# Twelve matmuls with unused results between the last V tiles of a decode attention kernel

## The chip, the cores and the metric

The kernel runs on one core of a Trainium2 chip (trn2). The metric is the device time of one execution in microseconds (us), given as the median of several. A profile comes from one of these executions. Its span runs from the first to the last instruction and is about 1.8 us shorter than the device time of that execution. In the profile PE is TensorE, PEld its weight loads, DVE VectorE, ACT ScalarE and POOL GpSimd; L192 is line 192 of the kernel. PSUM is the memory in which the kernel keeps the outputs of its matmuls (its pools with `space=bass.MemoryType.PSUM`).

## The reference

Attention for one new token: 32 query heads, 8 key/value heads (four query heads share one), 65536 positions, head size 128, all in bf16.

```python
B, Hq, Hkv, Sq, Sk, D = 1, 32, 8, 1, 65536, 128
k = jnp.repeat(k, rep, axis=1); v = jnp.repeat(v, rep, axis=1)   # rep = 4
scores = jnp.einsum("bhqd,bhkd->bhqk", q, k) * D ** -0.5
p = jax.nn.softmax(scores, axis=-1)
return jnp.einsum("bhqk,bhkd->bhqd", p, v)
```

K and V together are 268 MB, and every byte is used once. Little arithmetic is done per byte.

## The kernel before

The work goes group by group (one group is one K/V head). Each head's K and its V are read in four tiles of 4 MB each, called (g, s) below. So (7,0), (7,1), (7,2) and (7,3) are the last V tiles of the program. Five buffers hold tiles in flight. VectorE transposes K, TensorE forms the scores S, ScalarE takes the exponential, and TensorE multiplies with V. The very last tile is loaded in five pieces, so that little remains to be done once its last bytes land.

```python
iopool = ctx.enter_context(tc.tile_pool(name="iopool", bufs=5))
pss = ctx.enter_context(tc.tile_pool(name="pss", bufs=1, space=bass.MemoryType.PSUM))

CUTS = (T // 2, 3 * T // 4, 7 * T // 8, T - T // 16)      # T = 128 slots
EDGE = CUTS[-1]

def v_step(g, j):
    vt = load(v_view[g, j], "vt")
    # ...
    for c0 in range(0, CW, NQ):
        for u in range(2):
            wide(A[u], E, j, vh[u], u, c0, start=..., stop=...)   # 4 matmuls, 32 in all

def last_step(g, j):
    vt = load(v_view[g, j], "vt", CUTS)
    # ...
    W = pss.tile([P, HI * D], fp32, name="W", tag="S")
    first = halves(vt, 1)[0]
    for c0 in range(0, CW, NQ):                           # first half of the tile: 16 matmuls
        wide(W, E, j, first, 0, c0, start=(c0 == 0), stop=(c0 == CW - NQ))
    Rw = stats.tile([P, D], fp32, name="Rw")
    diagonal([(0, W)], Rw[:, :])                          # VectorE
    nc.vector.tensor_add(out=Rw[:, :], in0=Rw[:, :], in1=R[:, :D])
    # ...
    for t in range(CUTS[0], EDGE):                        # 56 small matmuls into Dp
        slot(t, Dp[s * QP:s * QP + HPG, :], ...)
    nc.vector.tensor_add(out=Ds[:, :], in0=Dp[:, :], in1=Rw[:, :])
    for t in range(EDGE, T):                              # 8 small matmuls into ps_f
        slot(t, ps_f[:, :], t == EDGE, False)
    nc.tensor.matmul(out=ps_f[:, :], lhsT=selh[:, :], rhs=Ds[:, :], start=False, stop=True)
    store(g, ps_f[:, :], rl[:, :], nc.sync)
```

## Time and profile before

| | before |
|---|---|
| device time, six runs | 634.11 us (633.81 to 634.24) |
| span of the profile | 632.4 us |
| HBM bytes read, mean rate | 268.47 MB, 425 GB/s |
| last V bytes released TensorE at | 628.5 us |

The chain of waits of the kernel before, cut to 560 us onward (start, length, what held things up):

```profile
555.77 43.38 DMA vt<-in_v_dram
...
599.17 29.32 DMA vt<-in_v_dram
628.48 0.04 issue
628.53 1.01 PE ps_f L271 x8
629.54 0.44 PE ps_f L283 x2
629.98 0.02 issue
630.01 0.34 DVE o L234
```

The end of the program waits for V loads until 628.48 us. After that come 1.45 us of matmuls, a scaling and the store.

The timeline of the kernel before shows TensorE at the last V tiles (start, length, engine, line, what; in brackets the idle time before and what ended it). The groups are tiles (7,0), (7,1), (7,2) and W, the first half of the last tile.

```profile
602.51 3.60 PE L192 MATMUL A<-vt,E 128*32 128x512 bf16 x32 [2.15 <-DVE rl L258]
...
608.90 2.48 PE L192 MATMUL A<-vt,E 128*32 128x512 bf16 x32 [2.79 <-DMA vt<-in_v_dram]
...
618.62 3.60 PE L192 MATMUL A<-vt,E 128*32 128x512 bf16 x32 [7.24 <-DMA vt<-in_v_dram]
...
623.53 1.90 PE L192 MATMUL W<-vt,E 128*32 128x512 bf16 x16 [1.30 <-DMA vt<-in_v_dram]
```

The same 32 matmuls took 1.91 us elsewhere in the program (from 553.81 and from 572.53 us, there at a granted clock of 1.00). They take 3.60 us at (7,0) and (7,2), where the granted TensorE clock is 0.50. The table by stage of the kernel before shows it (busy time of PE, PEld, DVE, ACT, POOL; then the granted clock, the DMA share and GB/s):

```profile
608.90:611.40 2.50, 2.48 (x32) 1.07 (x32) 0.00 (x0) 0.00 (x0) 0.00 (x0) 0.74 1.00 433
611.40:618.60 7.20, 0.00 (x0) 0.00 (x0) 0.00 (x0) 0.00 (x0) 0.00 (x0) 0.50 0.96 407
618.60:622.30 3.70, 3.60 (x32) 1.36 (x32) 0.45 (x1) 0.00 (x0) 0.00 (x0) 0.50 0.98 414
...
625.50:627.00 1.50, 1.00 (x32) 0.83 (x32) 1.47 (x2) 0.00 (x0) 0.00 (x0) 0.50 0.58 229
```

TensorE idles 7.2 us at clock 0.50, and works on at 0.50. The clock fell before that gap and not in it: during (7,1), at about 610.1 us (1.00 from 606.7 to 610.1 us, 0.50 from there to the end).

### The profile page before, as it was taken

How to read it: one execution, taken by the hardware profiler on the slowest of the kernel's cores; microseconds unless marked ns; L12 is line 12 of the kernel's file. 1: busy time of each engine (PE TensorE's matmuls, PEld its weight loads, DVE VectorE, ACT ScalarE, POOL GpSimd, SP SyncE). 2: the span in 40 equal slices, each digit the busy share in tenths (PEclk: the TensorE clock that was granted, in tenths of full speed). 3: DMA queues.
4: the chain of work that ended last, by engine and by line, in shares of the span. 5: the costliest groups of instructions: out<-in, count | busy, mean ns of one | idle time of the engine just before them, and what ended most of it. 6: DMA issues, size and time to landing. Idle time of an engine off the chain costs nothing.

```text
span 632.4 us, 4867 instructions
## 1 busy us (share of the span) xinstructions
PE 374.1 (59%) x2138; PEld 143.4 (23%) x2138; DVE 361.7 (57%) x234; ACT 17.8 (3%) x17; POOL 4.9 (1%) x7
## 2 busy tenths in 40 slices
PE   0586676747467474574745756458574566654635
PEld 0232222212122121221212222123121222211212
DVE  0898664675437763378634775347753477543713
ACT  0000100010000100001000010000100000000100
POOL 3000000000000000000000000000000000000000
PEclk9999698758887587876878967788686896778865
DMA  8999999999999999999999999999999999999995
GB/s 367 433 431 432 434 430 431 432 435 433 434 431 428 431 430 431 431 430 433 426 431 431 430 434 432 431 430 431 435 428 431 428 431 433 428 434 430 431 430 246
DMA packets 10069, 268.79 MB, mean 425 GB/s; under 512 B 1344, under 2 KB 1344, under 8 KB 1728
## 3 DMA queue, kind: packets, MB, share of 16 engines
q1 hardware_dynamic: 9800, 268.44, 98.9%
q8 instruction: 17, 0.28, 0.2%
q10 hardware_dynamic: 248, 0.04, 0.0%
q14 instruction: 4, 0.03, 0.0%
HBM read 268.47 MB, written 0.01 MB: 425 GB/s over the span
## 4 chain that ended last, share of the span: by engine, by line
DMA 58%; DVE 18%; PE 18%; issue 4%; ACT 0%; ACTq 0%; DVEq 0%
DMA kt<-in_k_dram 44%; PE S L143 15%; DVE kT L134 12%; DMA vt<-in_v_dram 11%; DMA q<-in_q_dram 2%; PE A L192 2%; DVE mx L154 2%; DVE E L179 1%; DVE R L228 1%; DVE t L222 1%; ACT ET L174 0%; PE ps_f L241 0%; DVE o L234 0%; DVE Z L118 0%; ACTq L235 0%
## 5 line engine op out<-in xcount | busy, mean ns | idle before, releaser
L143 PE MATMUL S<-kT,Z 128*128 128x512 bf16 x1024 | 296.0, 446 | 211.9 <-DVE kT L134 209.4
L134 DVE STREAM_TRANSPOSE kT<-kt 128x2048 int32<-128x2048 int32 x128 | 289.2, 2291 | 199.1 <-DMA kt<-in_k_dram 155.3
L143 PEld LDWEIGHTS <-Z 128*128 128x128 bf16 x1024 | 110.9, 109 | 395.3 <-issue 280.9
L192 PE MATMUL A<-vt,E 128*32 128x512 bf16 x992 | 66.4, 399 | 12.2 <-DMA vt<-in_v_dram 10.0
L192 PEld LDWEIGHTS <-E 128*32 128x32 bf16 x1008 | 26.0, 100 | 51.9 <-issue 29.7
L174 ACT ACTIVATE ET<-S,nm 128x2048 bf16<-128x2048 f32 x8 | 15.7, 1967 | 579.5 <-DVE nm L171 579.5
L154 DVE TENSOR_REDUCE mx<-S 128x1 f32<-128x2048 f32 x8 | 18.3, 2292 | 15.9 <-PE S L143 15.9
L179 DVE STREAM_TRANSPOSE E<-ET 128x2048 bf16<-128x2048 bf16 x8 | 18.5, 2312 | 9.2 <-ACT ET L174 9.2
L222 DVE TENSOR_TENSOR t<-A,mask 128x512 f32<-128x512 f32 x16 | 10.8, 680 | 19.4 <-PE A L192 19.4
L228 DVE TENSOR_REDUCE R<-t 128x128 f32<-128x1024 f32 x8 | 15.0, 1881 | 0.0
L169 PE MATMUL ps_b<-one,mrow 1*128 1x1 f32 x16 | 3.1, 258 | 11.3 <-DVE mrow L163 11.3
L241 PE MATMUL ps_f<-R,selh 128*4 128x129 f32 x14 | 3.7, 362 | 10.2 <-DVE nm L171 10.2
L108 DVE STREAM_TRANSPOSE qT<-q 128x64 int32<-128x64 int32 x1 | 0.2, 245 | 16.2 <-DMA q<-in_q_dram 16.2
L156 PE MATMUL ps_t<-ident,mx 128*1 128x128 f32 x8 | 2.2, 270 | 6.3 <-DVE mx L154 6.3
L169 PEld LDWEIGHTS ps_b<-one,mrow 1*128 1x128 f32 x16 | 2.6, 199 | 13.4 <-PE A L192 7.7
L112 POOL MEMSET Z<- 128x4992 bf16 x1 | 4.3, 4264 | 0.0
L234 DVE TENSOR_SCALAR o<-ps_f,rl 4x128 bf16<-4x128 f32 x8 | 2.7, 338 | 1.6 <-PE ps_f L283 1.4
L243 DVE RECIPROCAL rl<-ps_f 4x1 f32<-4x1 f32 x7 | 1.1, 155 | 4.3 <-PE ps_f L241 4.3
L241 PEld LDWEIGHTS ps_f<-R,selh 128*4 128x4 f32 x14 | 0.8, 83 | 10.6 <-issue 10.6
L156 PEld LDWEIGHTS ps_t<-ident,mx 128*1 128x1 f32 x8 | 0.6, 79 | 10.3 <-DVE mx L154 7.3
L271 PEld LDWEIGHTS <-E 128*4 128x4 bf16 x64 | 2.2, 111 | 2.5 <-issue 2.0
L192 PE MATMUL W<-vt,E 128*32 128x512 bf16 x16 | 1.9, 625 | 1.3 <-DMA vt<-in_v_dram 1.3
(28 smaller groups left out, 17.9 us busy)
## 6 DMA issues: line engine op xcount, KB each, us to landing
kt<-in_k_dram SPq DMA_DIRECT2D x32, 4096.0 KB, 43.2
vt<-in_v_dram SPq DMA_DIRECT2D x31, 4096.0 KB, 37.7
vt<-in_v_dram SPq DMA_DIRECT2D x1, 2048.0 KB
vt<-in_v_dram SPq DMA_DIRECT2D x1, 1024.0 KB
vt<-in_v_dram SPq DMA_DIRECT2D x1, 512.0 KB
vt<-in_v_dram SPq DMA_DIRECT2D x2, 256.0 KB
out_dram<-o ACTq DMA_DIRECT2D x7, 1.0 KB
q<-in_q_dram ACTq DMA_DIRECT2D x4, 8.0 KB, 6.3
```

Source lines behind the costliest of these rows:

```text
L112: nc.gpsimd.memset(Z[:, :, :, :, :], 0.0)
L134: nc.vector.transpose(out=kT[:, :].bitcast(i32), in_=kt[:, i2 * CW * D:(i2 + 2) * CW * D].bitcast(i32),)
L143: nc.tensor.matmul(out=S[:, j, :NCOL], lhsT=Z[:, b, e, g, w0:w0 + P], rhs=kT_v[:, i - i2, b, e, :, :], start=(i == 0 and be == 0), stop=(i ...
L154: nc.vector.reduce_max(out=mx[:, :], in_=S[:, :, :NCOL], axis=AX.XY)
L156: nc.tensor.transpose(out=ps_t[:, :], in_=mx[:, :], identity=ident[:, :])
L169: nc.tensor.matmul(out=ps_b[:, :], lhsT=mrow[:, :], rhs=one[:, :], start=True, stop=True)
L174: nc.scalar.activation(out=ET[:, :].rearrange("p (a n) -> p a n", a=NQ), in_=S[:, :, :NCOL], func=ACT.Exp, bias=nm[:, :], scale=SCALE, acc ...
L179: nc.vector.transpose(out=E[:, :, :, :].rearrange("p a c r -> p (a c r)"), in_=ET[:, :])
L192: nc.tensor.matmul(out=dst[s * QP:(s + 1) * QP, :], lhsT=E[:, j, c0 + s, :], rhs=v_half[:, :, c0 + s, :], start=start, stop=stop,)
L222: nc.vector.tensor_tensor(out=t[:, x * HI:(x + 1) * HI, :], in0=acc[:, :].rearrange("p (i d) -> p i d", i=HI), in1=mask[:, u * HI:(u + 1) ...
L228: nc.vector.tensor_reduce(out=out, in_=t[:, :n, :].rearrange("p i d -> p d i"), axis=AX.X, op=ALU.add,)
L241: nc.tensor.matmul(out=ps_f[:, :], lhsT=selh[:, :], rhs=R[:, :], start=True, stop=True)
```

## The change

The intent is to give TensorE something to do while it waits for the last loads, in the hope that its clock then stays up for the work after them: eight matmuls after tile (7,1), four after (7,2), into one half of a PSUM tile named spare; nobody reads that half. W moves into the other half.

```diff
-        W = pss.tile([P, HI * D], fp32, name="W", tag="S")
+        W = spare[:, 0, :]
...
+    def keep_busy(n):
+        for _ in range(n):
+            nc.tensor.matmul(
+                out=spare[:, 1, :], lhsT=Z[:, 0, 0, 0, :P],
+                rhs=Z[:, 1, :, :, :].rearrange("p e g z -> p (e g z)")[:, :512],
+                start=True, stop=True,
+            )
...
             v_step(g, s)
             if s == NQ - 1:
                 finish(g)
+            if g == Hkv - 1:
+                if s == 0:
+                    spare = pss.tile([P, 2, 512], fp32, name="spare", tag="S")
+                if s > 0:
+                    keep_busy((0, 8, 4)[s])
```

More of the change, by code (lines that the diff above doesn't have):

```diff
@@ L292 @@
                 softmax(g)
-        else:
-            if g == Hkv - 1 and s == NQ - 1:
-                last_step(g, s)
-            else:
-                v_step(g, s)
-                if s == NQ - 1:
-                    finish(g)
+        elif g == Hkv - 1 and s == NQ - 1:
+            last_step(g, s)
+        else:
+            v_step(g, s)
+            if s == NQ - 1:
+                finish(g)
+            if g == Hkv - 1:
[3 more added lines that the diff above has]
+                    keep_busy((0, 8, 4)[s])
 _INS = ['q', 'k', 'v']
```

## The prediction

> **What bounds the kernel now.** Loads. The page shows the DMA engines at 9 tenths in nearly every one of 40 slices, 268.47 MB read at a mean of 425 GB/s over a 632.4 us span. The chain of waits, cut to 560 us onward, is 72.7 us of V loads (two stretches, 43.38 and 29.32 us, back to back) until 628.48 us. Only then come eight matmuls into ps_f (1.01 us), the selh matmul (0.44 us), the scaling (0.34 us) and the store. About 1.5 us of that is TensorE work that a faster clock could shorten.
>
> **Clock in the tail.** In the stage table TensorE idles from 611.4 to 618.6 us (granted clock 0.50), and the clock stays at 0.50 from there to the end: tile (7,2) takes 3.60 us for 32 matmuls, where the V tiles at clock 1.00 took 1.90 us. [...] The change means to fill the gaps: 8 matmuls after tile (7,1), 4 after (7,2).
>
> **What the change really does.** The instruction order of the built kernel shows otherwise: the scheduler puts all twelve in one block, before tile (7,0), since they depend only on the release of S: the first waits for the Activation of the last softmax. None is left between the last V tiles. The other engines keep their order.
>
> **Cost.** The exp ends at about 600.1 us, so the block starts there, where TensorE now idles 2.15 us for the transpose of E. At the half clock this trace spaces 128x512 matmuls 0.427 us apart, so twelve take at most 5.1 us, an estimate; if the clock rises on the way, 3.8 to 4.5. The block then ends at 604 to 605.2 us. Tile (7,0) then starts 2 to 3 us later than its 602.51 us, probably at the full clock (1.9 us), at worst still at half (3.6 us). It ends between 606.3 and 609.2 us, against 606.1. Tile (7,1) is released by its load at 608.9 us, as before, and takes about 1.9 instead of 2.48 us.
>
> **How much is on the critical path.** None. The last load was issued at 599.2 us, before the block can begin, so no buffer is released later. From about 611 to 618.6 us TensorE idles as before, so the clock falls back to 0.50; (7,2), W and the last slots run as now. Even if the tail did run at the full clock, it would save half of 1.45 us, about 0.7 us or 0.1%.
>
> **Prediction.** 633.9 us, range 633.2 to 634.6. Faster by over 2%: 0.005; within 2%: 0.985; slower by over 2%: 0.01.
>
> **What would show it.** Right: in the timeline, twelve matmuls into spare in one block from about 600.1 us; granted clock higher at tiles (7,0) and (7,1); (7,2) starting within 1 us of 618.6 at 0.50 and taking about 3.6 us; the chain again V loads to about 628.5 us, then about 2 us of work; DMA at about 425 GB/s. Wrong: dummies seen between (7,1) and (7,2); (7,2) at 1.9 us; last V landing shifted by over 1 us.
>
> [...]

The forecast's sum is the time of the kernel before, put at 633.9 us, and nothing for the twelve matmuls. But the cut paragraph held the only reasons given why the time could differ, so the range of 633.2 to 634.6 us stands as an estimate without its reasons. The 3.8 to 4.5 us for the block are an estimate too: at 0.427 us for a matmul at clock 0.50 and half of that at 1.00 (V tiles took 3.60 and 1.90 us), twelve take so long if the clock rises after six to nine of them. When it would rise was not shown.

## More of the kernel before

The page of the kernel before has its DMA rows in 40 equal slices (busy tenths, then GB/s), and a table of the DMA queues.

```profile
span 632.4 us, 4867 instructions
...
DMA  8999999999999999999999999999999999999995
GB/s 367 433 431 432 434 430 431 432 435 433 434 431 428 431 430 431 431 430 433 426 431 431 430 434 432 431 430 431 435 428 431 428 431 433 428 434 430 431 430 246
...
q1 hardware_dynamic: 9800, 268.44, 98.9%
q8 instruction: 17, 0.28, 0.2%
```

The DMA engines are busy from end to end at about 431 GB/s. Only the first and the last slice are lower. The row "q8 instruction" looks like nothing: 17 transfers of about 16 KB.

## The result

| | before | after |
|---|---|---|
| device time, median of six runs | 634.11 us (633.81 to 634.24) | 633.98 us (633.82 to 634.30) |
| ratio after to before | | 0.9999, 95% interval 0.9986 to 1.0012 |

A ratio, here and below, compares the fast runs of both kernels within the same rounds, so it is not quite the ratio of the medians.

The timeline of the kernel after, TensorE at the same tiles. The first group is the block of twelve. Next come tiles (7,0) (its last 29 matmuls), (7,1) and (7,2), then W, which now lives in the tile named spare:

```profile
600.47 4.70 PE L291 MATMUL spare<-Z 128*128 128x512 bf16 x12 [1.53 <-ACT ET L174]
...
605.16 1.89 PE L192 MATMUL A<-vt,E 128*32 128x512 bf16 x29
...
608.72 1.91 PE L192 MATMUL A<-vt,E 128*32 128x512 bf16 x32 [1.67 <-DMA vt<-in_v_dram]
...
618.45 3.41 PE L192 MATMUL A<-vt,E 128*32 128x512 bf16 x32 [7.82 <-DMA vt<-in_v_dram]
...
623.36 1.05 PE L192 MATMUL spare<-vt,E 128*32 128x512 bf16 x16 [1.50 <-DMA vt<-in_v_dram]
```

All twelve ran before tile (7,0), released by ScalarE's exponential; none was left between the last tiles. Tiles (7,0) and (7,1) became faster. Both had slack, so each start after them is still set by a load: (7,2) begins after 7.82 us of idle time, at a slow clock again (1.00 until 614.7 us, 4.1 us into that idle time, then 0.50 until 621.5 us).

The chain of waits of the kernel after, cut to 560 us onward:

```profile
598.98 29.33 DMA vt<-in_v_dram
628.31 0.04 issue
628.36 1.01 PE ps_f L271 x8
629.37 0.44 PE ps_f L283 x2
629.81 0.02 issue
629.83 0.34 DVE o L234
```

This is the chain of before, with the same lengths. W's 1.05 us against 1.90 us needs a word, because it looks like a gain from the change. It is not one: a kernel without any unused matmul (e5_spare_only, below) also ran W in 1.05 us in its profile, while e7_skip_matmuls, with the twelve in place, ran it in 1.90 us. When the clock rises within those few microseconds differs from profile to profile: in the kernel after it rose at 621.5 us, in before it was 0.50 from 610.1 us to the end, in e7 0.50 from 618.4 us on. And W is not in the chain of waits.

### The profile page after: what moved, and what is told of

Its sections match the earlier page's. It is cut to its first block, busy times and chain, and to the rows that moved or that the text cites. A ratio compares the mean times of both kernels' runs of the same rounds, so it can differ in the third digit from the quotient of the medians.

```text
span 632.2 us, 4891 instructions
## 1 busy us (share of the span) xinstructions
PE 375.2 (59%) x2150; PEld 144.6 (23%) x2150; DVE 361.6 (57%) x234; ACT 17.7 (3%) x17; POOL 4.9 (1%) x7
## 4 chain that ended last, share of the span: by engine, by line
DMA 58%; DVE 17%; PE 17%; issue 6%; ACT 0%; ACTq 0%; DVEq 0%
DMA kt<-in_k_dram 45%; PE S L143 14%; DMA vt<-in_v_dram 12%; DVE kT L134 11%; DMA q<-in_q_dram 2%; PE A L192 2%; DVE mx L154 2%; DVE E L179 1%; DVE R L228 1%; DVE t L222 1%; ACT ET L174 0%; PE ps_f L241 0%; DVE o L234 0%; DVE Z L118 0%; ACTq L235 0%
## 5 line engine op out<-in xcount | busy, mean ns | idle before, releaser
L192 PE MATMUL A<-vt,E 128*32 128x512 bf16 x992 | 64.0, 388 | 9.5 <-DMA vt<-in_v_dram 9.5
L291 PE MATMUL spare<-Z 128*128 128x512 bf16 x12 | 4.7, 575 | 1.5 <-ACT ET L174 1.5
L271 PE MATMUL Dp<-vt,E 128*4 128x128 bf16 x56 | 2.0, 302 | 1.7 <-DMA vt<-in_v_dram 1.6
```

The source lines that it names most:

```text
L192: nc.tensor.matmul(out=dst[s * QP:(s + 1) * QP, :], lhsT=E[:, j, c0 + s, :], rhs=v_half[:, :, c0 + s, :], start=start, stop=stop,)
L291: nc.tensor.matmul(out=spare[:, 1, :], lhsT=Z[:, 0, 0, 0, :P], rhs=Z[:, 1, :, :, :].rearrange("p e g z -> p (e g z)")[:, :512], start=True ...
```

## The experiments

Theory A is the one of the prediction: the loads set the end, and TensorE has slack before 628 us. Rival B: the change is right, and only the scheduler's hoisting (it moved the matmuls ahead of tile (7,0)) hid its gain. Rival C: a busier TensorE slows the loads, and this ate a gain. Two more theories, D and E, were formed when an expectation fell.

### Matmuls that cannot be hoisted: e1_pinned12

```diff
-                rhs=Z[:, 1, :, :, :].rearrange("p e g z -> p (e g z)")[:, :512],
+                rhs=vt[:, lo:lo + 512],          # the V tile just used
...
-                    keep_busy((0, 8, 4)[s])
+                    keep_busy((0, 8, 4)[s], vt)
```

> The same twelve unused matmuls, but each reads the V tile just used, so the scheduler cannot move them ahead: 8 run after tile (7,1), 4 after (7,2), as the change intends. Theory A (loads set the end, TensorE has slack before 628 us): 633.9 us as before, within 0.3 us; the eight take about 1.7 us from 610.7 us, the clock still falls by 618.5 us because about 6 us of idle remain. Rival B (only the hoisting hid a gain): up to 0.7 us faster, near 633.3 us, with (7,2) at 1.9 us.

Measured: 633.40 us against 634.05 us of before. Four of five runs lie at 633.28 to 633.53 us and the fifth at 634.29 us; nine runs of before lie at 633.72 to 634.14 us, and one of the seven beside e5 to e7 at 633.51 us. The ratio is 0.9995 with an interval of 0.9981 to 1.0008, so a gain is not established. The profile (of the run of 633.28 us) shows what a gain would consist of. Timeline of e1_pinned12, from tile (7,2) on:

```profile
618.34 3.30 PE L192 MATMUL A<-vt,E 128*32 128x512 bf16 x32 [4.41 <-DMA vt<-in_v_dram]
621.58 1.28 PE L291 MATMUL spare<-vt,Z 128*128 128x512 bf16 x4
623.24 1.05 PE L192 MATMUL spare<-vt,E 128*32 128x512 bf16 x16 [0.38 <-DMA vt<-in_v_dram]
...
628.27 0.61 PE L272 MATMUL ps_f<-vt,E 128*4 128x128 bf16 x8 [0.36 <-DVE Ds L281]
628.72 0.38 PE L284 MATMUL ps_f<-Ds,selh 128*4 128x128 f32 x2
```

Tile (7,2) still ran at the half clock but for its first 0.4 us (the clock fell at 618.7 us), as theory A said: the eight matmuls left 4.41 us of the gap before it idle. The four after (7,2) made TensorE busy from 618.34 to 622.86 us without a gap. The clock rose at 622.1 us, and here it stayed at 1.0 to the end. In the chain of waits the eight last matmuls took 0.61 us instead of 1.01, and the selh matmul (the last one, which sums the partitions of each head) 0.23 instead of 0.44. That is 0.6 us of 634; another 0.26 us of the profile's 0.9 is that the eight start at 628.27 and not at 628.53 us. If this is a gain, it has the size that rival B foresaw, about a thousandth, at the limit of what the runs resolve. It does not come from (7,2), which took 3.30 us and not rival B's 1.9.

### Fill the gaps: e2_pinned_fill

The diff is against e1.

```diff
-                    keep_busy((0, 8, 4)[s], vt)
+                    keep_busy((0, 33, 12)[s], vt)
...
+        keep_busy(6, vt)                         # after W
```

> Enough pinned matmuls to fill the gaps: 33 after (7,1), about 7.1 us at the full clock, 12 after (7,2), 6 after W. Theory A: the clock is 1.0 for (7,2), 1.9 us, and W, 1.05 us, yet the last V load still lands at about 628.3 us; only the 1.45 us of matmuls after it can shrink, so the whole is 0 to 0.7 us faster. Rival B: a visible gain of 2 us or more from (7,2) and W running 2.5 us shorter. Rival C (busy TensorE slows the loads): last landing later than 629 us, GB/s below 420 in that stretch.

Measured: 633.77 us, between 633.40 and 634.67, ratio 1.0000. The profile is of the run of 634.67 us. In it (7,1) ran at the half clock in 3.61 us instead of 1.9, and the block after it ran partly cold and took 8.01 us instead of 7.1. Together this started (7,2) at 620.53 us, 2 us later than in the other kernels. The granted clock was 0.50 until 614.5 us, 5.8 us after TensorE had begun on (7,1). The expectation had sized the block at the full clock throughout. W came at 625.06 us, and VectorE, which waited for the last unused matmul before it could read W, began only at 627.55 us:

```profile
626.04 1.47 PE L292 MATMUL spare<-vt,Z 128*128 128x512 bf16 x6
627.55 0.69 DVE L223 TENSOR_TENSOR t<-spare,mask 128x512 f32<-128x512 f32 x1 [2.00 <-PE spare L292]
```

The end then hung on VectorE and not on the loads. The last V bytes were not later (the last V transfer ended at 627.8 us, in before at 628.1; TensorE is released about 0.4 us after that). Here, filling the gap to the brim turned waiting for a load into waiting for the filler (2.00 us of VectorE). No run shows rival B's 2 us, nor rival C's slower loads (407 and 402 GB/s in the stretches 611 to 618.4 and 618.4 to 622 us, against 410 and 411 of before, and the end of the loads unmoved).

### How much slack is there: e3_hoist48 and e4_hoist120

```diff
+            if g == Hkv - 1 and s == 0:
+                spare = pss.tile([P, 2, 512], fp32, name="spare", tag="S")
+                keep_busy(48)                    # e4: 120
             v_step(g, s)
...
-                    keep_busy((0, 8, 4)[s])
```

> 48 unused matmuls in one hoisted block before (7,0) in place of 12. Theory A: block from 600.5 to about 612.5 us, tiles (7,0) and (7,1) follow at the full clock until about 616.4 us, still before the load of (7,2) lands at 618.5 us: 633.9 us within 0.3 us, (7,2) at the full clock, 1.9 us. Rival C: 0.5 us or more slower.

> 120 unused matmuls in the hoisted block: the dose that must exceed the slack. Block about 27.6 us long, ends about 628 us; then three V tiles of 1.9 us, W 1.05 us, and the vector work of A and W (about 5.3 us) before the last matmul. Theory A: 8 to 11 us slower, TensorE now ends the chain, while the last V load still lands at about 628.3 us with the DMA rate unchanged. Rival C: the last landing moves later too.

Measured: 634.07 us with 48 (ratio 1.0002) and 644.00 us with 120 (ratio 1.0159, interval 1.0145 to 1.0172). With 48, tile (7,2) ran in 1.91 us at the full clock. Timeline of e3_hoist48:

```profile
618.42 1.91 PE L192 MATMUL A<-vt,E 128*32 128x512 bf16 x32 [2.80 <-DMA vt<-in_v_dram]
```

The time did not move: a tile 1.7 us shorter was worth nothing here, where TensorE next waits for a load (3.00 us before W). With 120, TensorE at last set the end of the program, followed by VectorE's sums over A and W. The chain of waits of e4_hoist120, cut to 600 to 632.7 us:

```profile
600.80 11.93 PE spare L291 x49
612.72 0.05 issue
612.78 10.74 PE spare L291 x49
623.52 0.05 issue
623.57 4.05 PE spare L291 x18
627.62 5.11 PE A L192 x92
```

No load stands in this chain from 600 us to the end. The DMA rate in the last 8 us before 628 us was 313 GB/s, against 318 of before, and the last V bytes landed at 627.9 us, so a TensorE busy without a break did not slow the loads. Rival C is out.

### One part alone, and what really sets the end: e5, e6, e7

```diff
# e5: no unused matmul, W in the spare tile
-                    keep_busy((0, 8, 4)[s])
+                    keep_busy((0, 0, 0)[s])
# e6: (7,2) is not loaded, its matmuls read (7,1) again
-        vt = load(v_view[g, j], "vt")
+        if (g, j) == (Hkv - 1, 2):
+            vt = reuse[0]
+        else:
+            vt = load(v_view[g, j], "vt")
+        reuse[:] = [vt]
# e7: (7,2) is loaded, 24 of its 32 matmuls are left out
+            if (g, j) == (Hkv - 1, 2) and c0 < CW - NQ:
+                continue
```

> One part of the change alone: W lives in a half of the spare tile, no unused matmul runs. Theory A: 633.9 us within 0.4 us, tile (7,0) back at 602.5 us, at the half clock. If the two parts had cancelled, this alone would be 0.5 us or more away from before.

> Wrong result on purpose: the load of tile (7,2), 4.19 MB, is left out, and its matmuls read tile (7,1) again. All TensorE work stays. Theory A: shorter by 4.19 MB over 431 GB/s, 9.7 us, so about 624.2 us. If TensorE set the end, 0 to 2 us shorter.

> Wrong result on purpose: tile (7,2) is loaded, but 24 of its 32 matmuls are left out, which takes about 2.6 us off TensorE in the gap that the change aims at, more than a doubled clock could. Theory A: 633.9 us within 0.4 us. Rival B: 1.5 to 2.6 us faster.

Measured, against 634.14 us of before: e5 634.17 us (ratio 1.0002), e6 624.37 us (0.9847), e7 634.11 us (1.0002). The three start from the kernel after, so e6 and e7 keep the twelve matmuls; e6 and e7 give wrong results. A load of 4.19 MB taken away is worth 9.77 us, which is its bytes over the rate. Three quarters of the same tile's matmuls taken away are worth nothing. The chain of waits of e6_skip_load, then the timeline of e7_skip_matmuls at (7,2) and at the last matmuls:

```profile
589.34 29.33 DMA vt<-in_v_dram
...
618.72 1.01 PE ps_f L277 x8
```

```profile
618.59 1.05 PE L192 MATMUL A<-vt,E 128*32 128x512 bf16 x8 [7.79 <-DMA vt<-in_v_dram]
...
628.49 1.01 PE L273 MATMUL ps_f<-vt,E 128*4 128x128 bf16 x8 [0.26 <-DMA vt<-in_v_dram]
```

Without its load the same end comes 9.8 us sooner. With (7,2) at 1.05 us, less than the 1.9 us of the full clock, the end waits for the loads as before. No clock could do more for that tile than e7 did.

### Try to build the faster version: e8, e9, e10

e8 keeps the clock up from (7,2) to the end, with the 48 of e3 and 11 pinned ones after (7,2). e9 takes work off the end in another way: it loads the last piece in two, so that 4 matmuls follow the last bytes instead of 8. e10 is both.

```diff
# e8, e10
+                keep_busy(48, Z[:, 1, :, :, :]...)   # before (7,0)
...
-                    keep_busy((0, 8, 4)[s])
+            if g == Hkv - 1 and s == NQ - 2:
+                keep_busy(11, vt[:, :512])           # after (7,2)
# e9 (on the kernel before), e10
-    CUTS = (T // 2, 3 * T // 4, 7 * T // 8, T - T // 16)
+    CUTS = (T // 2, 3 * T // 4, 7 * T // 8, T - T // 16, T - T // 32)
```

> The 48 hoisted matmuls, which brought (7,2) to the full clock, and 11 pinned ones after (7,2), about 2.4 us, to hold it until W's load lands at 623.3 us; none later. If the clock is worth only the TensorE work after the last landing: clock 1.0 from (7,2) to the end in nearly every execution, W 1.05 us, last load still at 628.2 to 628.4 us, the end 0.6 to 0.8 us sooner, 633.3 us. If the good runs of the pinned twelve had another cause: 633.9 us or more.

> The kernel before, no unused matmul, but the last 8 slots (two loads of 256 KB at the end) become 4 and 4 (256, 128 and 128 KB): after the last landing 4 matmuls at the half clock instead of 8. Theory A: 4 times 0.107 us, 0.4 us faster, if the smaller transfers land no later; if they do, 0 to 0.3 us slower.

> Both together. The two act on the same 1.45 us, so less than the sum: 0.7 to 0.9 us faster than before, near 633.2 us; if either lever fails alone, it shows here as the other alone.

Measured, against 634.06 us: e8 635.29 us (ratio 1.0020, interval 1.0008 to 1.0033), e9 633.68 us (0.9996, interval 0.9982 to 1.0009), e10 635.01 us (1.0015, interval 1.0001 to 1.0028). e9 lies where it was expected, inside the noise; its four last matmuls took 0.59 us, where the eight of before took 1.01 (0.105 us for each of the four saved). e8 and e10 are a miss: expected 0.7 us or more faster, measured 1.2 and 1.0 us slower. The timeline of e8_warm_tail shows that the clock did what it should up to 629.8 us, and something else went wrong:

```profile
623.37 1.05 PE L192 MATMUL spare<-vt,E 128*32 128x512 bf16 x16 [0.51 <-DMA vt<-in_v_dram]
...
627.09 0.40 PE L272 MATMUL Dp<-vt,E 128*4 128x128 bf16 x16 [0.64 <-DMA vt<-in_v_dram]
...
629.18 0.28 PE L272 MATMUL Dp<-vt,E 128*4 128x128 bf16 x8 [1.70 <-DMA vt<-in_v_dram]
```

W is as quick as hoped, but TensorE waits 1.70 us for a piece of V that in e1 let it go on at 627.63 us (e10 waits 1.76 us at the same place). A load is late, and only at the very end. After the wait the clock is lost again, at 629.8 us: the eight last matmuls took 0.96 us. The list of single transfers in the trace shows what stands before it: one 16 KB transfer of the "instruction" kind, which lasted 1.11 us. It ran from 627.0 us on, in front of the last V transfers of its DMA engine. The first of those V transfers starts as it ends, at 628.1 us, and the last one lands at 629.3 us, 1.4 us after all others. In the kernel before, the same kind of transfer came at 628.9 us, behind the last V bytes. What these transfers bring is inferred from the trace of before: the profile calls their kind "instruction", and from the first of the 17, at 50.1 us, to the last, at 628.9 us, TensorE executed 4074 instructions (2037 matmuls and as many weight loads), about 255 to each 16 KB transfer, and VectorE only 199. So this queue is taken to be TensorE's, and each transfer to be a fetch of its next instructions.

This gave theory D: unused matmuls are also instructions. The 118 added ones (59 matmuls with a weight load each) would have moved a fetch from behind the last load to in front of it. Rival E: the pinned matmuls themselves delay the loads.

### Instructions without unused matmuls in the tail: e12_before_pad59, and e11_warm_pad69

e12 is the kernel before with 59 tiny matmuls (118 instructions) at the very start, done by 2.7 us, when TensorE has nothing to do until 22 us. e11 is e8 with 69 of them.

```diff
+    pz = const.tile([P, QP], bf16)
+    nc.vector.memset(pz[:, :], 0.0)
+    pp = psm.tile([QP, 16], fp32, name="pp", tag="misc")
+    for _ in range(59):                              # e11: 69
+        nc.tensor.matmul(out=pp[:, :], lhsT=pz[:, :], rhs=pz[:, :16], start=True, stop=True)
```

> The kernel of the 48 hoisted and 11 pinned matmuls, which came out 1.2 us slower with its last V byte 1.3 us late, plus 69 tiny matmuls (138 instructions) at the very start, where TensorE waits until 22 us anyway. With the 118 it has already, that is 256 more than the kernel before, one 16 KB fetch of instructions. Theory D (a fetch of TensorE's instructions landed in front of the last V transfers on their DMA engine): the fetch moves behind the last V byte again, which lands at 628.2 to 628.5 us; clock 1.0 to the end; 633.3 us, 0.7 us faster than before. Rival E (the pinned matmuls themselves delay the loads): still 635.2 us, landing at 629.7 us.

> The kernel before, untouched but for 59 tiny matmuls (118 instructions) at the very start, so that its tail lies as far along in the instruction stream as that of the slow kernel with 48 + 11. No unused matmul in the tail. Theory D: the last fetch of TensorE's instructions starts before the last V byte, by 1 to 2.5 us, and the time is 1.0 to 1.4 us above before, 635.1 to 635.5 us. Rival E: 634.0 us within 0.3 us.

Measured, against 634.00 us: e12 635.36 us (ratio 1.0022, interval 1.0008 to 1.0035; five runs, 635.05 to 635.72, none near the nine of before). Theory D's number came out, without one unused matmul in the tail. So the pinned matmuls are not needed for the delay, and rival E is not its explanation. (The tiny matmuls also need a small tile in SBUF, 64 bytes per partition, and may shift what lies behind it; that was not tried by itself, but e8 and e10 are late in the same way without it.) In the trace the fetch of e12 lasts from 627.05 to 628.16 us, and from then on V transfers come only one after the other, to 629.08 us, as in e8. And the pads at the start do move this queue: its first transfer comes at 35.4 us and not at 50.1.

A fetch before the last V byte is not enough, though. In e3, with 96 more instructions than before, the last fetch began at 627.6 us, and in e2, with 102 more, at 627.5 us; the last V bytes landed at 627.9 and 627.8 us, and were not late. The two fetches ended at 628.7 and 628.6 us, after those bytes, so no V transfer had waited behind them. What seems to count is whether V transfers stand behind the fetch on its own engine.

The timeline of e12_before_pad59 has the late piece:

```profile
627.13 1.03 PE L277 MATMUL Dp<-vt,E 128*4 128x128 bf16 x24 [0.22 <-DMA vt<-in_v_dram]
...
629.55 1.01 PE L277 MATMUL ps_f<-vt,E 128*4 128x128 bf16 x8 [1.40 <-DMA vt<-in_v_dram]
```

The DMA view of e12_before_pad59 (queue, kind: transfers, MB, share of 16 engines) from 627 to 628 us has the fetch among the V transfers:

```profile
q1 hardware_dynamic: 64, 0.11, 28.8%
q8 instruction: 1, 0.02, 6.9%
```

and the same view of the kernel before, from 628.5 to 629.5 us, has the fetch alone, after the V transfers:

```profile
q8 instruction: 1, 0.02, 7.4%
```

e11 did not bring the time back: 635.05 us (ratio 1.0017, interval 1.0004 to 1.0029). Its last fetch did go behind the last V byte, as theory D said. But the V pieces were late from W on: W waited until 624.75 us instead of 623.4. The view of e11_warm_pad69 from 619 to 621 us has another fetch there,

```profile
q1 hardware_dynamic: 68, 0.73, 87.7%
q8 instruction: 1, 0.02, 3.3%
```

where the kernel before has none; its own lies at about 612 us, and its V pieces were not late. So e11's expectation failed. What fits is that any fetch in the last 10 us or so can hit; but why a fetch at 612 us costs nothing while one near 620 us seems to cost 1.3 us stays open. One observation may bear on it. If each transfer in the trace is matched with the one that starts as it ends, 16 chains come out, one per DMA engine. In the kernel before, seven of them have finished their V bytes some 3 us before the other nine. A fetch on an early one would then delay no V byte, which no run tried. The matching is a reconstruction, and the trace does not name the engines.

## Why the prediction was right

- **The loads bound the kernel: shown.** Predicted were 633.9 us, measured 633.98. e6 took 4.19 MB away and 9.77 us went; e7 took 24 matmuls of the same tile away and nothing went.
- **All twelve run in one block before (7,0): right.** The prediction said 600.1 us and an end between 604 and 605.2 us; the timeline has 600.47 us and 4.70 us, an end at 605.2 us.
- **(7,0) 2 to 3 us later at the full clock, (7,1) in 1.9 us: right.** (7,0) began at 605.1 us (2.6 us later), and (7,1) took 1.91 us.
- **Nothing of it on the critical path: right.** The chain has the same pieces before and after. e3 shows that even four times the dose is hidden, e4 that ten times is not.
- **"(7,2), W and the last slots run as now": right in effect, not in detail.** (7,2) took 3.41 us, but W ran at the full clock. That is not due to the twelve, since in e5 W ran in 1.05 us without any unused matmul. It cost nothing and gained nothing.
- **At most 0.7 us from a tail at the full clock: held as a size.** The one profile with such a tail throughout and nothing late (e1) shows 0.6 us. That this is a gain in the median is not proven.
- **What the prediction did not think of.** It counted the added matmuls by their time alone. As instructions they move the fetches. The change added 24 and its fetch still fell behind the last V byte: in the trace the last V bytes land at 627.9 us and the fetch starts at 628.05 us, where in before it was 628.1 and 628.9 us. The 96 of e3 cost nothing either; with 118 it cost 1.2 to 1.4 us (e8, e12), more than the warm clock could give. So the prediction was right here by a margin that it had not looked at; that part was luck.

Left open: whether e1 or e9 beats the kernel before by their 0.4 to 0.6 us, and whether the last loads can be spread better. In the kernel before, the DMA engines are only 0.58 busy at 229 GB/s from 625.5 to 627 us, while V is still being waited for. About 3 us at that share leave room for some 1.3 us, an estimate from (1 − 0.58) × 3 us, which no run tried. What makes the clock fall is not settled either. In the kernel after it fell 4.1 us into the 7.82 us of idle time before (7,2); in e8 it stayed at 1.00 over gaps of 1.41 and 1.70 us; but in before it fell at 610.1 us, during (7,1), after only 2.79 us of idle time.

## What to carry to other kernels

Before warming an engine up, ask what its next instruction waits for: here even a tile 1.7 us shorter was worth nothing, because a load came next. Of TensorE's work only the 1.45 us behind the last load could gain. Look at the built order before believing where an instruction without dependencies stands, and tie it to data if it must stand there. And instructions were not free here even when their engine idled: they shift the instruction fetches, and 118 of them, with one fetch in front of the last V transfers, cost 1.2 to 1.4 us (e8, e12), about twice the 0.6 to 0.7 us that the clock could have gained.
